# A fused two-layer kernel with Mish on one core: two x tiles by DMA transpose, and half of the first weight load issued later

## The chip, the cores and the metric

The kernel runs on one core of a Trainium2 chip. The metric is the device time of one execution in microseconds (us). Five engines work beside each other: TensorE (PE in the profile; its weight loads are PEld), VectorE (DVE), ScalarE (ACT), GpSimd (POOL) and SyncE (SP). Each runs its own instructions in order and waits on semaphores. SP and ScalarE also hand transfers to the 16 DMA engines, each through a queue of its own.

## What is computed

x is 2048 x 512, w1 is 512 x 1792, b1 has 1792 elements, w2 is 1792 x 512; all are bf16.

```python
h = jnp.einsum("bsd,df->bsf", x, w1) + b1
sp = jnp.log1p(jnp.exp(-jnp.abs(h))) + jnp.where(h > 0, h, jnp.zeros_like(h))
act = h * jnp.tanh(sp)            # Mish
return jnp.einsum("bsf,fd->bsd", act, w2)
```

## The kernel before

The 2048 rows of x are cut into four blocks of 512 rows. For each block the first layer is computed transposed: for each of 14 tiles f of 128 hidden columns, four matmuls (k = 0 to 3, the four parts of 128 of the inner dimension 512) add up in one PSUM bank, with the weights w1[k, f] stationary and x transposed streaming (512 columns). ScalarE applies Mish with the bias and writes a_sb (line 156). Then the second layer: for each of the block's four row tiles i, fourteen matmuls over f (line 189) with 512 columns of w2, a copy by VectorE (line 195), and a store issued on SP (line 198). All loads are issued at the start; nothing is loaded twice.

x is needed transposed (the tensor xT: 128 partitions of the inner dimension, by k, by row). Blocks 1 to 3 get it by a DMA transpose, issued on SP after all other loads (line 113, through the helper at line 84). Block 0 is needed first and gets it by TensorE: its four row tiles of 128 rows (x0 to x3 below) are loaded plainly into x_nat on SP (x0, x1 singly, x2 and x3 in one load, lines 101 to 103), transposed by TensorE into PSUM in four pieces of 128 x 128 each (`transpose_x`, line 134, transposes at line 144), and copied to xT by VectorE and ScalarE in turn (line 148).

w1 for the first four f (F0 = 4) is loaded on ScalarE's queue in two halves of 256 KB, k 0-1 and then k 2-3 (lines 99 and 100). Behind the x tiles, SP's queue has b1 (line 104), w1 for f 4-7 and for f 8-13 (lines 105, 106), w2 whole (line 107) and the three DMA transposes.

Around the change the order of the work is written out by hand (lines 214 to 239). TensorE first runs six matmuls on constants (line 127), then transposes x0, then alternates: `first(js, ks)` computes, for the four f of F0, the parts k in `ks` of the row tiles in `js`, in PSUM banks 4 to 7. So k 0 of x0 is done while x1 is not there yet, and 512 columns are put together from pieces of 128 and 256. The order before is:

```python
first((0,), (0,)); transpose_x(1); first((0,), (1,)); first((1,), (0, 1)); first((0, 1), (2,))
transpose_x(2); transpose_x(3); first((0, 1), (3,)); first((2, 3), (0, 1))
# bias: 14 x 128 transposed by TensorE (line 231)
first((2, 3), (2, 3))
```

When k 3 of the last row tile is done, Mish follows for that f. Then come f 4 to 13 in 512 columns (line 237) and the second layer of block 0 (line 239). The waits in the code are explicit: `Stream.wait` puts a semaphore wait into the engine's own instruction order, so what stands behind it on that engine waits too.

Of the kernel before, what the change touches and what calls it, by code (L numbers as in the profile page):

```python
# [5 lines left out]
P = 128  # L6
# [25 lines left out]
def bass_standalone__dense_activation_mish__prompt_kernel(  # L32
# [10 lines left out]
    BF, F32 = dt.bfloat16, dt.float32  # L43

    _, S, D = x.shape
    F = w1.shape[1]
    KT, FT = D // P, F // P
    assert (S, D, F) == (2048, 512, 1792) and sum(BLOCKS) == S
    x2, out2 = x[0], out[0]
# [3 lines left out]
    F0 = 4  # L53
    N0 = BLOCKS[0] // P

    with ExitStack() as es:
        def sb(name, shape, t):
            return es.enter_context(nc.sbuf_tensor(name, shape, t))

        x_nat = sb("x_nat", [P, N0, D], BF)  # L60
        xT = sb("xT", [P, KT, S], BF)
        w1_sb = sb("w1_sb", [P, KT, F], BF)
        w2_sb = sb("w2_sb", [P, FT, D], BF)
# [9 lines left out]
        def sem(name):  # L73
            return es.enter_context(nc.semaphore(name))

        sp = Stream(nc.sync, None)
        pe = Stream(nc.tensor, sem("c_pe"))
        dve = Stream(nc.vector, sem("c_dve"))
        act = Stream(nc.scalar, sem("c_act"))
        pool = Stream(nc.gpsimd, sem("c_pool"))  # L80

        def load(q, dst, src, name, transpose=False):
            s = sem(name)
            (q.eng.dma_start_transpose if transpose else q.eng.dma_start)(dst, src).then_inc(s, 16)
            return (s, 16)

        def load_w1(q, ks, a, b):
            return load(q, w1_sb[:, ks, a * P:b * P], w1v[:, ks, a * P:b * P], "s_w1_%d_%d" % (ks.start, a))


        t_xn, t_w1, t_w2 = [None] * N0, {}, {}

        def load_part(q, k0, k1, a, b):
            t = load_w1(q, slice(k0, k1), a, b)
            for f in range(a, b):
                for k in range(k0, k1):
                    t_w1[k, f] = t

        for k0, k1 in ((0, 2), (2, 4)):
            load_part(act, k0, k1, 0, F0)  # L100
        for j in range(2):
            t_xn[j] = load(sp, x_nat[:, j, :], x2[j * P:(j + 1) * P, :], "s_xn%d" % j)
        t_xn[2] = t_xn[3] = load(sp, x_nat[:, 2:4, :], x2[2 * P:4 * P, :].rearrange("(j p) d -> p j d", p=P), "s_xn2")
        t_b1 = load(sp, b1_nat[:, :], b1.rearrange("(j p) -> j p", p=P), "s_b1")
        load_part(sp, 0, KT, 4, 8)
        load_part(sp, 0, KT, 8, FT)
# [21 lines left out]


        free = [[] for _ in range(8)]  # L130
        t_cp = {}
        t_mish = {}

        def transpose_x(j, banks):

            pe.wait(t_xn[j], t_id)
            n = KT // len(banks)
            for h, bank in enumerate(banks):
                eng = (dve, act)[h % 2]
                pe.wait(*free[bank])  # L140
                psb = ps[:, bank, 0:n * P // 2].bitcast(BF)
                for i in range(n):
                    k = n * h + i
                    mm = nc.tensor.transpose(psb[:, i * P:(i + 1) * P], x_nat[:, j, k * P:(k + 1) * P], ident[:, :])  # L144
                eng.wait(pe.mark(mm))
                dst = xT[:, n * h:n * h + n, j * P:(j + 1) * P]
                src = psb.rearrange("p (k t) -> p k t", k=n)
                t = eng.mark(nc.vector.tensor_copy(dst, src) if eng is dve else act.eng.activation(dst, src, ACT.Copy))  # L148
                for i in range(n):
                    t_cp[j, n * h + i] = t  # L150
                free[bank] = [t]

        def mish(s, f, bank, t_mm):
            n = BLOCKS[s]
            act.wait(t_b1c, t_mm)
            t = act.mark(act.eng.activation(a_sb[:, f, starts[s]:starts[s + 1]], ps[:, bank, 0:n], ACT.Mish,  # L156
                                            bias=b1_sb[:, f:f + 1]))
            t_mish[s, f] = t
            free[bank] = [t]

        def mm1_step(s, f, k, bank, js=None):

            n = BLOCKS[s]
            lo, hi = (0, n) if js is None else (js[0] * P, (js[-1] + 1) * P)
            first = k == 0 and lo == 0
            if first:
                pe.wait(*free[bank])
            pe.wait(t_w1[k, f])
            if s:
                pe.wait(t_xT[s])  # L170
            else:
                pe.wait(*[t_cp[j, k] for j in (js or range(N0))])
            return nc.tensor.matmul(ps[:, bank, lo:hi], w1_sb[:, k, f * P:(f + 1) * P],  # L173
                                    xT[:, k, starts[s] + lo:starts[s] + hi], start=first, stop=(k == KT - 1 and hi == n))
# [32 lines left out]
        def first(js, ks):  # L207
            for k in ks:
                for f in range(F0):
                    mm = mm1_step(0, f, k, 4 + f, js)  # L210
                    if k == KT - 1 and js[-1] == N0 - 1:
                        mish(0, f, 4 + f, pe.mark(mm))
# [4 lines left out]
        dummy(256)  # L217
        first((0,), (0,))
        transpose_x(1, (0, 1))
        first((0,), (1,))  # L220
        first((1,), (0, 1))
        first((0, 1), (2,))
        transpose_x(2, (2, 3))
        transpose_x(3, (0, 1))
        dve.wait(t_b1, t_bz)
        t_b1p = dve.mark(nc.vector.tensor_copy(b1_pad[0:FT, :], b1_nat[:, :]))  # L226
        first((0, 1), (3,))
        first((2, 3), (0, 1))
        pe.wait(t_b1p, *free[2])
        psb1 = ps[:, 2, 0:P // 2].bitcast(BF)  # L230
        t_b1t = pe.mark(nc.tensor.transpose(psb1, b1_pad[:, :], ident[:, :]))  # L231
        dve.wait(t_b1t)
        t_b1c = dve.mark(nc.vector.tensor_copy(b1_sb[:, :], psb1[:, 0:FT]))  # L233
        free[2] = [t_b1c]
        first((2, 3), (2, 3))
        for f in range(F0, FT):
            mm1(0, f, {4: 0, 5: 1, 6: 2, 7: 3}.get(f, 4 + f % 4))
        for i in range(N0):
# [40 lines left out]
```

## Time and profile before

| | us |
|---|---|
| median of 3 runs | 106.08 |
| lowest and highest | 105.43, 106.5 |
| the profiled execution, its own time | 105.33 |
| its span, first to last instruction | 104.1 |
| TensorE busy in the span | 101.2 |
| ScalarE busy | 40.4 |
| VectorE busy | 12.8 |

The profile is one execution. The span is shorter than the time of the execution by 1.2 us, which lies around the instructions. Times within the profile count from the start of the span. A row of the timeline gives start, length, engine, line, operation and what it writes and reads, with the idle time before it and what ended that idle time. The chain of work that ended last is followed back from the last instruction, at each step to what released it; its pieces are listed in order of time. A busy TensorE is not TensorE at its peak, since matmuls overlap in its pipeline: the rate is read from the start of one to the start of the next.

### The profile page before, as it was taken

How to read it: one execution, taken by the hardware profiler on the slowest of the kernel's cores; microseconds unless marked ns; L12 is line 12 of the kernel's file. 1: busy time of each engine (PE TensorE's matmuls, PEld its weight loads, DVE VectorE, ACT ScalarE, POOL GpSimd, SP SyncE). 2: the span in 40 equal slices, each digit the busy share in tenths (PEclk: the TensorE clock that was granted, in tenths of full speed). 3: DMA queues.
4: the chain of work that ended last, by engine and by line, in shares of the span. 5: the costliest groups of instructions: out<-in, count | busy, mean ns of one | idle time of the engine just before them, and what ended most of it. 6: DMA issues, size and time to landing. Idle time of an engine off the chain costs nothing.

```text
span 104.1 us, 1166 instructions
## 1 busy us (share of the span) xinstructions
PE 101.2 (97%) x510; PEld 48.1 (46%) x510; DVE 12.8 (12%) x25; ACT 40.4 (39%) x62; POOL 0.7 (1%) x6
## 2 busy tenths in 40 slices
PE   6999999999999999999999999999999999999992
PEld 2486444444444444444444444444444444444462
DVE  0220000022220000022220000022112000011223
ACT  3426987000027777200007777500005777700000
POOL 2000000000000000000000000000000000000000
DMA  2999999941101000010111000001111000001111
GB/s 66 337 341 378 349 202 210 270 122 50 45 6 50 0 0 6 0 50 3 48 50 50 0 3 0 6 0 50 50 50 50 0 0 0 0 6 50 50 50 50
DMA packets 12689, 7.94 MB, mean 76 GB/s; under 512 B 6796, under 2 KB 12684, under 8 KB 12684
## 3 DMA queue, kind: packets, MB, share of 16 engines
q1 hardware_dynamic: 12140, 7.35, 25.6%
q10 hardware_dynamic: 544, 0.52, 1.5%
q8 instruction: 4, 0.07, 0.2%
q14 instruction: 1, 0.01, 0.0%
HBM read 4.20 MB, written 2.10 MB: 60 GB/s over the span
## 4 chain that ended last, share of the span: by engine, by line
PE 94%; DMA 3%; DVE 1%; issue 0%
PE ps L173 47%; PE ps L189 47%; DMA w_sb<-in_w_dram 3%; PE ps L144 1%; DVE xT L148 0%; DVE o_sb L195 0%; PE ps L231 0%
## 5 line engine op out<-in xcount | busy, mean ns | idle before, releaser
L156 ACT ACTIVATE a_sb<-ps,b_sb 128x512 bf16<-128x512 f32 x56 | 37.6, 690 | 46.1 <-PE ps L173 46.0
L173 PE MATMUL ps<-xT,w_sb 128*128 128x512 bf16 (+2 forms) x248 | 49.7, 359 | 0.2
L189 PE MATMUL ps<-w_sb,a_sb 128*128 128x512 bf16 (+2 forms) x238 | 49.0, 367 | 0.0
L173 PEld LDWEIGHTS ps<-xT,w_sb 128*128 128x128 bf16 x248 | 23.4, 98 | 25.4 <-DMA w_sb<-in_w_dram 0.4
L189 PEld LDWEIGHTS ps<-w_sb,a_sb 128*128 128x128 bf16 x238 | 22.8, 98 | 25.9
L195 DVE CAST o_sb<-ps 128x512 bf16<-128x512 f32 (+2 forms) x17 | 11.2, 660 | 83.0 <-PE ps L189 83.0
L127 PE MATMUL ps<-const-bfloat16-1.0 128*128 128x512 bf16 (+1 forms) x7 | 2.9, 557 | 0.8 <-PEq L264 0.8
L148 ACT ACTIVATE xT<-ps 128x256 bf16<-128x256 bf16 (+1 forms) x5 | 1.5, 340 | 2.5 <-PE ps L144 2.5
L121 ACT ACT_TABLE_LOAD x1 | 1.3, 1283 | 1.8 <-issue 1.8
L148 DVE COPY xT<-ps 128x256 bf16<-128x256 bf16 (+1 forms) x5 | 1.2, 265 | 4.6 <-PE ps L144 4.6
L127 PEld LDWEIGHTS ps<-const-bfloat16-1.0 128*128 128x128 bf16 x7 | 0.9, 135 | 1.9 <-issue 1.9
L144 PE MATMUL ps<-ident,x_nat 128*128 128x128 bf16 x16 | 1.6, 243 | 0.0
L144 PEld LDWEIGHTS ps<-ident,x_nat 128*128 128x128 bf16 x16 | 1.1, 108 | 0.7 <-DMA x_nat<-in_x_dram 0.7
L233 DVE CAST b_sb<-ps 128x14 f32<-128x14 bf16 x1 | 0.2, 173 | 1.2 <-PE ps L231 1.2
L119 POOL TENSOR_SCALAR_AFFINE_SELECT ident<-ones 128x128 bf16<-128x128 bf16 x1 | 0.3, 292 | 0.1
L116 DVE MEMSET b_pad<- 128x64 uint32 x1 | 0.1, 112 | 0.9 <-PEq L264 0.9
L231 PE MATMUL ps<-ident,b_pad 128*128 128x128 bf16 x1 | 0.2, 219 | 0.0
L117 POOL MEMSET ones<- 128x128 bf16 x1 | 0.2, 204 | 0.3 <-POOLq L264 0.3
L226 DVE COPY b_pad<-b_nat 14x128 bf16<-14x128 bf16 x1 | 0.2, 173 | 0.0
L231 PEld LDWEIGHTS ps<-ident,b_pad 128*128 128x128 bf16 x1 | 0.1, 98 | 0.0
L264 POOL MEMSET const-bfloat16-1.0<- 128x1 bf16 x1 | 0.1, 101 | 0.0
L264 POOL MEMSET const-uint8-127<- 128x1 uint8 x1 | 0.1, 101 | 0.0
(2 smaller groups left out, 0.2 us busy)
## 6 DMA issues: line engine op xcount, KB each, us to landing
out_dram<-o_sb SPq DMA_DIRECT2D x15, 128.0 KB, 1.7
w_sb<-in_w_dram SPq DMA_DIRECT2D x1, 1792.0 KB, 12.7
w_sb<-in_w_dram SPq DMA_DIRECT2D x1, 768.0 KB, 7.2
w_sb<-in_w_dram ACTq DMA_DIRECT2D x2, 256.0 KB, 3.7
w_sb<-in_w_dram SPq DMA_DIRECT2D x1, 512.0 KB, 5.5
x_nat<-in_x_dram SPq DMA_DIRECT2D x2, 128.0 KB, 2.7
x_nat<-in_x_dram SPq DMA_DIRECT2D x1, 256.0 KB, 4.0
out_dram<-o_sb SPq DMA_DIRECT2D x1, 96.0 KB, 1.6
```

Of the source, the lines that this page charges most:

```text
L117: t_ones = pool.mark(pool.eng.memset(ones[:, :], 1.0))
L119: t_id = pool.mark(pool.eng.affine_select(ident[:, :], ones[:, :], pattern=[[1, P]], compare_op=ALU.is_equal, fill=0.0, base=0, channel_mu ...
L121: act.eng.preload_act_table(ACT.Mish)
L127: nc.tensor.matmul(ps[:, 7, 0:n], c_w, c_m[:, 0:n], start=True, stop=True)
L144: mm = nc.tensor.transpose(psb[:, i * P:(i + 1) * P], x_nat[:, j, k * P:(k + 1) * P], ident[:, :])
L148: t = eng.mark(nc.vector.tensor_copy(dst, src) if eng is dve else act.eng.activation(dst, src, ACT.Copy))
L156: t = act.mark(act.eng.activation(a_sb[:, f, starts[s]:starts[s + 1]], ps[:, bank, 0:n], ACT.Mish, bias=b1_sb[:, f:f + 1]))
L173: return nc.tensor.matmul(ps[:, bank, lo:hi], w1_sb[:, k, f * P:(f + 1) * P], xT[:, k, starts[s] + lo:starts[s] + hi], start=first, stop=( ...
L189: return nc.tensor.matmul(ps[:, bank, 0:hi - lo], a_sb[:, f, i * P:(i + 1) * P], w2_sb[:, f, lo:hi], start=(f == 0), stop=(f == FT - 1))
L195: t = dve.mark(nc.vector.tensor_copy(o_sb[:, i, lo:hi], ps[:, bank, 0:hi - lo]))
L226: t_b1p = dve.mark(nc.vector.tensor_copy(b1_pad[0:FT, :], b1_nat[:, :]))
L231: t_b1t = pe.mark(nc.tensor.transpose(psb1, b1_pad[:, :], ident[:, :]))
```

## The change

x2 and x3 of block 0 are no longer loaded plainly, transposed by TensorE and copied. One DMA transpose, the third transfer on SP's queue, writes both into xT; x_nat keeps two tiles. ScalarE issues only k 0-1 of w1 at the start; the issue of k 2-3 stands behind the copies of x0 and x1 in ScalarE's order, with a wait for the landing of k 0-1. In the order of the work, k 0-1 is done in pieces as before (x0, x1, then x2 and x3 together), and k 2 and k 3 in 512 columns for all four row tiles, with the bias transpose between them.

```diff
-        x_nat = sb("x_nat", [P, N0, D], BF)
+        x_nat = sb("x_nat", [P, 2, D], BF)
...
-        for k0, k1 in ((0, 2), (2, 4)):
-            load_part(act, k0, k1, 0, F0)
+        load_part(act, 0, 2, 0, F0)
         for j in range(2):
             t_xn[j] = load(sp, x_nat[:, j, :], x2[j * P:(j + 1) * P, :], "s_xn%d" % j)
-        t_xn[2] = t_xn[3] = load(sp, x_nat[:, 2:4, :], x2[2 * P:4 * P, :].rearrange("(j p) d -> p j d", p=P), "s_xn2")
+        t_x23 = load(sp, xT[:, :, 2 * P:4 * P], x2[2 * P:4 * P, :], "s_x23", True)
         t_b1 = load(sp, b1_nat[:, :], b1.rearrange("(j p) -> j p", p=P), "s_b1")
...
-        t_cp = {}
+        t_cp = {(j, k): t_x23 for j in (2, 3) for k in range(KT)}
...
         first((0,), (0,))
         transpose_x(1, (0, 1))
+        act.wait(t_w1[0, 0])
+        load_part(act, 2, 4, 0, F0)
         first((0,), (1,))
         first((1,), (0, 1))
-        first((0, 1), (2,))
-        transpose_x(2, (2, 3))
-        transpose_x(3, (0, 1))
         dve.wait(t_b1, t_bz)
         t_b1p = dve.mark(nc.vector.tensor_copy(b1_pad[0:FT, :], b1_nat[:, :]))
-        first((0, 1), (3,))
         first((2, 3), (0, 1))
+        first(range(N0), (2,))
         pe.wait(t_b1p, *free[2])
...
-        first((2, 3), (2, 3))
+        first(range(N0), (3,))
```

More of the change, by code (lines that the diff above doesn't have):

```diff
@@ L88, in load_w1 @@
             return load(q, w1_sb[:, ks, a * P:b * P], w1v[:, ks, a * P:b * P], "s_w1_%d_%d" % (ks.start, a))
-        t_xn, t_w1, t_w2 = [None] * N0, {}, {}
+        t_xn, t_w1, t_w2 = [None] * 2, {}, {}
         def load_part(q, k0, k1, a, b):
```

## The prediction

> **What bounds the kernel now.** I read the page first, then the chain of work that ended last.
>
> ```profile
> PE 101.2 (97%) x510; PEld 48.1 (46%) x510; DVE 12.8 (12%) x25; ACT 40.4 (39%) x62; POOL 0.7 (1%) x6
> ...
> PE 94%; DMA 3%; DVE 1%; issue 0%
> ```
>
> TensorE is busy for 97% of the span, and the chain is TensorE but for 3% of DMA. So only what TensorE has to do, or has to wait for, can move the end. The chain in order of time shows where its waits lie:
>
> ```profile
> 0.80 3.21 DMA w_sb<-in_w_dram
> 4.01 0.04 issue
> 4.05 0.40 PE ps L173 x4
> ...
> 4.47 0.30 PE ps L144 x2
> ...
> 4.79 0.30 DVE xT L148
> ...
> 5.14 1.06 PE ps L173 x12
> 6.20 0.45 PE ps L144 x8
> 6.64 1.40 PE ps L173 x12
> 8.04 0.06 PE ps L231
> 8.10 9.51 PE ps L173 x48
> 17.60 12.09 PE ps L189 x56
> 29.69 12.09 PE ps L173 x56
> ```
>
> From 5.14 on TensorE never stops. All that the change touches lies before 8.97, where the last 40 of the 48 matmuls at 8.10 begin (f 4 to 13, 512 columns each). One 512-column matmul costs 12.09/56 = 0.216 us, so one of 256 columns costs 0.108. What happens to the end is the shift of the moment, now 17.60, at which the second layer begins. The queues that feed this, from the timeline:
>
> ```profile
> 0.80 0.99 ACTq L84 DMA_DIRECT2D w_sb<-in_w_dram  x2
> 0.81 1.35 SPq L84 DMA_DIRECT2D x_nat<-in_x_dram  x3
> ...
> 2.74 1.50 SPq L84 DMA_DIRECT2D w_sb<-in_w_dram  x3
> ...
> 4.27 15.76 SPq L84 DMA_TRANSPOSE xT<-in_x_dram  x3
> ...
> 4.90 0.38 ACT L148 ACTIVATE xT<-ps 128x256 bf16<-128x256 bf16 x1 [0.82 <-PE ps L144]
> 5.14 0.78 PEld L173 LDWEIGHTS ps<-xT,w_sb 128*128 128x128 bf16 x12 [0.22 <-DVE xT L148]
> ```
>
> The three issues from 2.74 (w1 for f 4-7, w1 for f 8-13, w2) are 0.5 apart: 2.74, 3.24, 3.74. Issue rows say when an engine hands a transfer over, not when it lands. Landings are in the page's DMA part, and in the views of the tiles w_sb, x_nat and xT, each with the least, median and longest:
>
> ```profile
> w_sb<-in_w_dram SPq DMA_DIRECT2D x1, 1792.0 KB, 12.7
> w_sb<-in_w_dram SPq DMA_DIRECT2D x1, 768.0 KB, 7.2
> w_sb<-in_w_dram ACTq DMA_DIRECT2D x2, 256.0 KB, 3.7
> w_sb<-in_w_dram SPq DMA_DIRECT2D x1, 512.0 KB, 5.5
> ```
> ```profile
> DMA to landing us min/median/max: 3.2/5.5/12.7
> ```
> ```profile
> DMA to landing us min/median/max: 2.3/3.2/4.0
> ```
> ```profile
> L84 SPq DMA_TRANSPOSE xT<-in_x_dram x3: 2027/2613/11032, 4.3 to 18.0; - x3
> ...
> DMA to landing us min/median/max: 4.1/4.8/14.0
> ```
>
> The two 256 KB loads of w1 on ScalarE's queue average 3.7; the first took 3.2 (0.80 to 4.01), so the second, k 2-3, took 4.2 and was there at about 5.5. TensorE first needs it at about 5.7. Today it is hidden.
>
> **The change part by part.**
>
> TensorE's work. The eight transposes of x tiles 2 and 3 go. Sixteen 256-column matmuls of k 2-3 become eight of 512: the same columns, so nothing. If no transfer were late, TensorE would go on at 5.14 with eight 128-column matmuls (their weight loads: 0.78/12 = 0.065 each, 0.52), be at 5.66, do x tiles 2-3 with k 0-1 (8 x 0.108 = 0.86), k 2, the bias transpose (0.06) and k 3 (8 x 0.216 = 1.73) and start f 4 at 8.31 instead of 8.97: a gain of 0.65. That is the most the removed work is worth. The four copies removed from VectorE and ScalarE lie beside TensorE and are worth nothing on the path. ScalarE's first queue stretch loses one issue (0.5), so its table load moves up; nothing waits for that.
>
> The start. Can x0, x1 and k 0-1 (512 KB) land sooner without the other loads?
>
> ```profile
> 1.60:3.20 1.60, 1.60 (x6) 0.51 (x5) 0.00 (x0) 1.28 (x1) 0.00 (x0) 1.00 0.76 228
> 3.20:4.00 0.80, 0.74 (x6) 0.41 (x5) 0.44 (x2) 0.41 (x2) 0.00 (x0) 1.00 1.01 337
> ```
>
> By 3.2 us 228 x 1.6 = 365 KB had moved; the 524 (thousand bytes) of these three need until 3.67 even if nothing else ran. So k 0-1 gains between 0 and 0.3. They were already first in their queues, and I take 0.
>
> x tiles 2-3 by DMA transpose, issued third on SP, at 1.73. Landing: the rows for double the bytes are 4.1 to 4.8, with less than 1 us to save for half the bytes. Bounds 3.2 and 4.8; I take 4.1, the row without other work before it: 5.8. TensorE then does the k 0-1 part until 5.83 + 0.86 = 6.7.
>
> SP's queue. The issue replaces one of 0.43; three issues of 512 rows took 2.0, 2.6 and 11.0, so half as many rows cost about 1.3, and between 0.4 and 2.7 (if, like the 11.0, it ends only when the data ahead is out, here near 4.4). Everything behind it on SP (bias, w1 for f 4-7 and 8-13, w2, the other transposes) is issued 0.9 later, bounds 0 to 2.3. On the wire these follow one another anyway. What changes there is a seam: at the one place where transposed data follows plain data now, the DMA engines moved almost nothing for 2 us.
>
> ```profile
> 14.50:15.00 0.50, 0.50 (x4) 0.21 (x3) 0.00 (x0) 0.37 (x1) 0.00 (x0) 1.00 0.83 65
> 15.00:15.50 0.50, 0.50 (x5) 0.20 (x3) 0.00 (x0) 0.45 (x1) 0.00 (x0) 1.00 2.92 36
> 15.50:16.00 0.50, 0.50 (x4) 0.27 (x3) 0.00 (x0) 0.32 (x2) 0.00 (x0) 1.00 0.08 8
> 16.00:16.50 0.50, 0.50 (x4) 0.22 (x3) 0.00 (x0) 0.50 (x1) 0.00 (x0) 1.00 0.45 96
> 16.50:18.00 1.50, 1.50 (x9) 0.69 (x7) 0.00 (x0) 1.15 (x3) 0.00 (x0) 1.00 1.28 288
> ```
>
> The last number is GB/s. So every later transfer lands 0.2 us (262 thousand bytes at 288 instead of 360 or so) to 2.2 later; after only 2 us of traffic I take 0.6. w2 now lands at 3.74 + 12.7 = 16.4 and is first used at 17.60: 1.2 of cover. w1 for f 4-7 lands at 2.74 + 5.5 = 8.2 and is used at 8.97: 0.7. Both uses move later too (below), so both stay hidden; without that move w2 at its upper bound, 18.6, would be next to stop TensorE. The bias copy on VectorE waits for a small load that now lies behind the transpose; its consumer comes after k 2, so it is hidden.
>
> k 2-3 on ScalarE. This is the term that decides. ScalarE works in order: the wait for k 0-1 and the issue stand behind its copy of x1, which ended at 4.90 + 0.38 = 5.28. By then k 0-1 has long landed, so the wait itself is free, but the load is issued at 5.28 instead of 1.3. Behind it on ScalarE is nothing until the first activation. Landing: 2.3 is the lowest row of any load here (half the bytes), 4.2 the same load in traffic; the nearest is k 0-1, same queue and size, 3.2. So 5.28 + 3.2 = 8.5, bounds 7.6 and 9.4.
>
> [...]
>
> The sum. TensorE waits from 6.7 to 8.5, then has 48 x 0.216 + 0.06 = 10.43 to do: second layer at 8.52 + 10.43 = 18.95 instead of 17.60, +1.35. Seen from the gain of 0.65, the late k 2-3 costs 2.0. The profiled execution took 105.33, with a span of 104.1, 0.75 under the median of 106.08; 105.33 + 1.35 = 106.7, and against the median 107.4. Break-even is a landing of k 2-3 at 17.60 - 10.43 - 0.04 = 7.13. With the bounds 7.6 and 9.4 this case runs from 106.5 to 108.4.
>
> **The rivals.**
>
> Early: k 2-3 lands before 7.6. For it: x1's copy may end up to 0.3 earlier, and TensorE has 0.65 to give back. Against it: 7.13 would need 1.85 from issue to landing, less than any load row. It decides below 7.13: no slower, at best 105.4, which is the end on the other side; between 7.13 and 7.6 up to 106.5.
>
> Backlog: the load is served in order of issue after SP's earlier ones. Behind w1 for f 8-13, which now lands at 3.24 + 7.2 = 10.4 and would land 0.2 to 0.8 later, it lands at 10.6 to 11.2: +3.5 to +4.1, 109.6 to 110.2. For it: x0, k 0-1, x1 and k 2-3 landed (3.1, 4.0, 4.4, 5.5) in about the order of issue. [...]
>
> Blocked issue: SP's first transpose for block 1 stays in issue for 11.0 us, until 15.3. If ScalarE can issue nothing during it, k 2-3 lands at 15.5 + 3.2 = 18.7, +11.6: 117.7. It decides if that transpose starts before ScalarE's 5.28; it starts at 4.27 now, 5.2 by my shift, up to 6.6. Landing behind w2 instead gives 16.6 and 115.5. Against it: the issues of ScalarE and SP at 0.80 and 0.81 ran side by side. [...]
>
> Clock: TensorE stands idle for 1.8 us and comes back slow.
>
> ```profile
> 1.22 0.15 PEld L127 LDWEIGHTS ps<-const-bfloat16-1.0 128*128 128x128 bf16 x1 [0.28 <-issue]
> 1.65 0.15 PEld L127 LDWEIGHTS ps<-const-bfloat16-1.0 128*128 128x128 bf16 x1 [0.28 <-issue]
> ```
>
> At the start the 512-column matmuls follow each other at 0.43, half speed, until somewhere before 4.05: up to 3.2 us, a loss of half of it, 1.6. Then 109.0. [...]
>
> **How the numbers follow.** Chances: forecast 0.58, early 0.10, backlog 0.10, blocked or behind w2 0.14, clock 0.08. The time is that of the likeliest, 107.4. The range 106.3 to 110.2 holds the forecast's own range (106.5 to 108.4), clock, backlog and the upper half of early; left out are 0.14 and about 0.05. A measurement here can tell about 1% (1.06 us) from no change. Slower by over 1% means a landing after 8.19: 0.34 of the forecast's 0.58, and backlog, blocked and clock, 0.66. Faster by over 1% would need more than the whole 0.65 and a sooner start: 0.02. The rest, 0.32, is within 1%.
>
> **What the changed profile would show.** Right: a wait of TensorE for w_sb of 1 to 3 us, ending near 8.5, ahead of the first 512-column matmul of line 173 in block 0; ScalarE's second issue near 5.3; no other new wait; the second layer at about 18.9. The transposed x tiles land between 4.9 and 6.5; later than 7.6 would make them the wait instead. Wrong: no wait for w_sb and the second layer at 17.0 (early); a landing past 10 (backlog, blocked); 512-column matmuls 0.43 apart after the wait (clock); a wait for w_sb at line 189 (w2's cover gone).

## The result, and the profile after

The changed kernel takes 113.23 us (median of 4 runs, 112.62 to 113.81) against 106.22 for the kernel before (4 runs): 1.069 times as long, 95% interval 1.064 to 1.074. The forecast was 107.4 with a range of 106.3 to 110.2. Ratios, here and below, leave out single runs that lay more than 1.5% above the fastest of their kernel. The profiled execution took 112.77, its span is 111.5 (before: 105.33 and 104.1).

From the profile of the changed kernel: busy time, the row of the granted TensorE clock by slices of 2.8 us, and the shares of the chain.

```profile
PE 103.6 (93%) x494; PEld 48.3 (43%) x494; DVE 12.4 (11%) x23; ACT 40.2 (36%) x60; POOL 0.7 (1%) x6
...
PEclk9997559999999999999999999999999999999999
...
PE 91%; DMA 6%; DVE 0%; issue 0%; ACT 0%
```

TensorE fell from 97% to 93% of the span, and a row for the clock has appeared: seven, five and five tenths between about 8 and 17 us. The chain in order of time says where the span grew.

```profile
5.20 0.01 ACT xT L147
5.20 7.23 DMA w_sb<-in_w_dram
...
12.48 1.89 PE ps L172 x4
14.36 0.11 PE ps L229
14.47 10.53 PE ps L172 x44
25.00 12.09 PE ps L188 x56
```

The second layer of block 0 begins at 25.00 instead of 17.60: 7.40 later, which is the whole growth of the span (111.5 - 104.1). From 25.00 on every piece has the length that it had before. Ahead of it there is one wait: k 2-3 of w1 is issued at 5.20 and lands at 12.43, 7.2 us later. The waits name the same thing, and their totals show that there is no other new wait for data on TensorE.

```profile
PEld ps L172 <- DMA w_sb<-in_w_dram: 5.9, 2, 5.5
PE ps L172 <- DMA w_sb<-in_w_dram: 5.2, 1, 5.2
```

The second part of the loss is what happens after the wait. The timeline of the weight loads:

```profile
12.47 0.13 PEld L172 LDWEIGHTS ps<-xT,w_sb 128*128 128x128 bf16 x2 [5.50 <-DMA w_sb<-in_w_dram]
...
12.88 0.15 PEld L172 LDWEIGHTS ps<-xT,w_sb 128*128 128x128 bf16 x1 [0.28 <-issue]
13.30 0.15 PEld L172 LDWEIGHTS ps<-xT,w_sb 128*128 128x128 bf16 x1 [0.28 <-issue]
```

They follow each other at 0.42, where a 512-column matmul at full clock takes 0.216. The stretches of the windows view (PE busy, PEld, DVE, ACT, POOL, granted clock, DMA share, GB/s) show from when to when:

```profile
7.00:7.30 0.30, 0.26 (x3) 0.00 (x0) 0.00 (x0) 0.00 (x0) 0.00 (x0) 1.00 1.06 375
7.30:9.00 1.70, 0.00 (x0) 0.00 (x0) 0.00 (x0) 0.00 (x0) 0.00 (x0) 1.00 1.06 382
9.00:10.00 1.00, 0.00 (x0) 0.00 (x0) 0.00 (x0) 0.00 (x0) 0.00 (x0) 0.80 1.07 387
10.00:11.00 1.00, 0.00 (x0) 0.00 (x0) 0.00 (x0) 0.00 (x0) 0.00 (x0) 0.50 1.07 349
...
14.00:16.40 2.40, 2.40 (x8) 0.86 (x7) 0.17 (x1) 1.40 (x3) 0.00 (x0) 0.50 1.23 277
16.40:17.60 1.20, 1.20 (x7) 0.61 (x6) 0.00 (x0) 1.20 (x3) 0.00 (x0) 0.99 1.18 267
```

TensorE stopped at 7.26; the clock fell to half at about 9.6 (0.80 is the mean of a stretch that is full for six tenths of it) and came back at 16.4. Note the last column as well: during TensorE's wait the DMA engines move 350 to 390 GB/s. They are not idle; they are moving something else.

The sum with these numbers: TensorE needs 10.43 after the landing at full clock, 12.48 + 10.43 = 22.91, so the clock cost 25.00 - 22.91 = 2.09 (with the restart after the wait, some 0.16 of it: with the clock kept, the same work takes 10.59 in an experiment below, 12.89 to 23.48). The landing came 12.43 - 8.48 = 3.95 later than forecast. Forecast shift 1.35 + 3.95 + 2.09 = 7.39.

What was moved in that time, from the list of issues with size and time to landing, and SP's issues:

```profile
w_sb<-in_w_dram SPq DMA_DIRECT2D x1, 1792.0 KB, 11.9
w_sb<-in_w_dram SPq DMA_DIRECT2D x1, 768.0 KB, 6.8
...
w_sb<-in_w_dram SPq DMA_DIRECT2D x1, 512.0 KB, 4.9
```
```profile
1.73 1.31 SPq L84 DMA_TRANSPOSE xT<-in_x_dram  x1
...
3.74 1.50 SPq L84 DMA_DIRECT2D w_sb<-in_w_dram  x3
...
5.20 0.37 ACTq L84 DMA_DIRECT2D w_sb<-in_w_dram  x1
5.29 15.56 SPq L84 DMA_TRANSPOSE xT<-in_x_dram  x3
```

w1 for f 4-7 is issued at 3.74 and lands at 8.6, w1 for f 8-13 is issued at 4.19 and lands at 11.0, w2 is issued at 4.73 and lands at 16.6. ScalarE's load comes after all three, lands behind two of them and ahead of the third. That is the suspicion with which the experiments begin.

### The profile page after: what moved, and what is told of

It reads as the page before. It is cut to its first block, busy times and chain, and to the rows that moved or that the text cites. A ratio compares the mean times of both kernels' runs of the same rounds, so it can differ in the third digit from the quotient of the medians.

```text
span 111.5 us, 1128 instructions
## 1 busy us (share of the span) xinstructions
PE 103.6 (93%) x494; PEld 48.3 (43%) x494; DVE 12.4 (11%) x23; ACT 40.2 (36%) x60; POOL 0.7 (1%) x6
## 4 chain that ended last, share of the span: by engine, by line
PE 91%; DMA 6%; DVE 0%; issue 0%; ACT 0%
PE ps L172 44%; PE ps L188 43%; DMA w_sb<-in_w_dram 6%; PE ps L126 2%; PE ps L143 1%; DVE o_sb L194 0%; PE ps L229 0%; ACT xT L147 0%
## 5 line engine op out<-in xcount | busy, mean ns | idle before, releaser
L155 ACT ACTIVATE a_sb<-ps,b_sb 128x512 bf16<-128x512 f32 x56 | 38.1, 688 | 54.6 <-PE ps L172 54.4
L172 PE MATMUL ps<-xT,w_sb 128*128 128x512 bf16 (+2 forms) x240 | 52.2, 380 | 5.2 <-DMA w_sb<-in_w_dram 5.2
L172 PEld LDWEIGHTS ps<-xT,w_sb 128*128 128x128 bf16 x240 | 23.9, 103 | 32.3 <-DMA w_sb<-in_w_dram 5.9
L194 DVE CAST o_sb<-ps 128x512 bf16<-128x512 f32 (+2 forms) x17 | 11.2, 660 | 84.1 <-PE ps L188 84.1
L147 ACT ACTIVATE xT<-ps 128x128 bf16<-128x128 bf16 (+1 forms) x3 | 0.9, 314 | 2.1 <-PE ps L143 2.1
L147 DVE COPY xT<-ps 128x128 bf16<-128x128 bf16 (+1 forms) x3 | 0.7, 247 | 3.5 <-PE ps L143 3.5
```

What stands on the lines that cost most here:

```text
L194: t = dve.mark(nc.vector.tensor_copy(o_sb[:, i, lo:hi], ps[:, bank, 0:hi - lo]))
```

## The experiments

Two theories: **backlog** (what SP has handed over earlier is moved first, whichever queue the later load uses) and **transpose** (the new DMA transpose in front is what holds the load up). The clock is a third matter, tested by itself. In the diffs, `rest of SP` stands for the loads of w1 for f 4-13, w2 and the three block transposes. Where a kernel was timed only once, the text says so, and what is read there is the landing in its profile.

**Undo the late issue, keep the DMA transpose.**

```diff
+        load_part(act, 2, 4, 0, F0)          # right behind k 0-1 at the start
...
-        act.wait(t_w1[0, 0])
-        load_part(act, 2, 4, 0, F0)
```

> The changed kernel with both halves of w1 for f 0-3 issued on ScalarE at the start again; x2 and x3 still by DMA transpose. Theory backlog (a load of ScalarE is moved only after what SP had handed over before it): no wait for w1; the transposed x tiles stand behind k 2-3 on the wire and land near 6.4 instead of 5.8, the second layer begins at 17.6 to 17.9, time 105.8 to 106.8. Theory transpose (the DMA transpose of the x tiles holds up what comes after it): TensorE waits for w1 of f 4-7 near 9, and the time is above 107.

Measured: 105.77 (10 runs) against 106.20, ratio 0.997 (0.994 to 0.9995). The chain of this kernel has no wait for w1 after the start:

```profile
5.14 3.37 PE ps L173 x24
8.50 0.06 PE ps L228
8.56 9.50 PE ps L173 x44
18.06 12.09 PE ps L189 x56
```

The second layer stands at 18.06 in this execution, a little past the expected 17.9; the median lies at the lower end of what was expected. That the layer begins later here than in the profile before (17.60), while the median is no longer, fits the matmul rates of the two executions: here the matmuls run at half rate until 7.0, in the profiled execution before only until somewhere before 4.05. So the DMA transpose, with everything that it moves on SP's queue, costs nothing that can be measured. The whole loss belongs to the late issue, as the next kernel shows.

**The late issue alone, in the kernel before.**

```diff
-        for k0, k1 in ((0, 2), (2, 4)):
-            load_part(act, k0, k1, 0, F0)
+        load_part(act, 0, 2, 0, F0)
...
         transpose_x(1, (0, 1))
+        act.wait(t_w1[0, 0])
+        load_part(act, 2, 4, 0, F0)
```

> The kernel before with one edit: k 2-3 of w1 is issued behind the copies of x1 with the wait for k 0-1. No DMA transpose for block 0. Theory backlog: k 2-3 lands after w1 for f 8-13 again, between 10 and 13; TensorE needs it at 5.7, so the second layer moves by 4.5 to 7 and more with a slow clock: 111 to 115. Theory transpose: without the early DMA transpose it lands 3.2 after its issue, near 8.5, +2.8: about 109.

Measured: 113.96, ratio 1.075 (1.069 to 1.082). There is no DMA transpose of x tiles in this kernel, and the load still takes 6.75:

```profile
4.85 6.75 DMA w_sb<-in_w_dram
...
26.33 12.09 PE ps L188 x56
```

It also answers the question of the blocked issue. SP's first block transpose was handed over at 4.28, before ScalarE's load, and stayed in issue for 11.5 us (view of xT: the least, median and longest issue in ns, first and last start):

```profile
L84 SPq DMA_TRANSPOSE xT<-in_x_dram x3: 1916/2012/11491, 4.3 to 17.8; - x3
```

ScalarE issued at 4.85, in 0.37, and its load landed at 11.60: SP's stuck issue did not stop it.

The theory transpose falls. The loss is as large as that of the whole change.

**SP holds its large loads until ScalarE has issued k 2-3.**

```diff
         act.wait(t_w1[0, 0])
         load_part(act, 2, 4, 0, F0)
+        sp.wait(t_cp[1, 2])                  # ScalarE's copy of x1
+        rest of SP                           # moved here from the start
```

> The changed kernel, but SP hands over w1 for f 4-13, w2 and the block transposes only when ScalarE's copy of x1 is done, which is just after ScalarE has issued k 2-3. Theory backlog: k 2-3 lands 2.6 to 3.2 after its issue, at 7.9 to 8.5, the second layer at 18.4 to 19.0, time 107.0 to 107.7 (the forecast's own case). Theory transpose (the x tiles' DMA transpose, still ahead, is what holds it up): it lands past 10 again and the time stays above 110.

Measured: 106.79 (9 runs), ratio 1.008 (1.004 to 1.011). The load is as late as in the changed kernel (here 5.57), behind the same DMA transpose, on the same queue. Only what lies ahead of it is gone:

```profile
5.57 2.80 DMA w_sb<-in_w_dram
...
19.03 12.09 PE ps L179 x56
```

2.8 instead of 7.2. That is the backlog, shown by removing it. It is also the case that the forecast had assumed, and the time lies inside that case's own range (106.5 to 108.4), though a little under the 107.0 that I expected here: the medians differ by 0.6, while the second layer is 1.43 later than in the profile before, which is of a short execution (105.33).

**How much of the backlog counts.** Three kernels, each timed once: with only w1 for f 4-7 ahead of the load, then w1 for f 4-13, then w2 in the place of w1 for f 8-13:

```diff
# first: hold from w1 for f 8-13 on; second: hold from w2 on (as above, sp.wait later in SP's order)
# third, nothing held:
         load_part(sp, 0, KT, 4, 8)
-        load_part(sp, 0, KT, 8, FT)
         t = load(sp, w2_sb[:, :, :], w2v, "s_w2")
+        load_part(sp, 0, KT, 8, FT)
```

> The changed kernel, but SP hands over w1 for f 8-13 and all behind it only after ScalarE's copy of x1; only w1 for f 4-7 (512 KB) is ahead of k 2-3. Theory limited order (the DMA engines work off what was handed over first, up to a certain number of pieces, and only then take turns between the two queues): k 2-3 lands after w1 for f 4-7, at 8.2 to 8.9. Theory turns (the queues take turns at once, and it is the sheer number of bytes in flight that slows the load): 7.8 to 8.2, ahead of w1 for f 4-7.

> As the run before, but w1 for f 4-7 and for f 8-13 (1280 KB) are both ahead of k 2-3, and only w2 is held. Theory limited order: k 2-3 lands after w1 for f 8-13, and sooner than the 12.4 of the changed kernel, where it shared with w2: 10.7 to 11.7. Theory turns: 7.8 to 8.5, as in the run before.

> The changed kernel with w2 handed over on SP before w1 for f 8-13; only the landing of k 2-3 is looked at, TensorE then waits for w1 as well. Theory limited order by pieces (ahead of k 2-3 lie w1 for f 4-7 and f 8-13, 64 pieces for each DMA engine, and w2 is where the sharing began): now w1 for f 4-7 and the first two sevenths of w2 are ahead, smaller pieces, so k 2-3 starts earlier, shares with the rest of w2 and lands at 11.0 to 12.0. Theory order by whole transfers (two are worked off, the third shares): behind all of w2, 14 or later.

Measured, the load's row in the chain of each of the three, in this order:

```profile
5.06 3.99 DMA w_sb<-in_w_dram
```
```profile
5.32 6.54 DMA w_sb<-in_w_dram
```
```profile
5.29 7.82 DMA w_sb<-in_w_dram
```

Issue to landing is 2.8 with nothing ahead, 4.0 behind 512 KB (landing 9.05, after w1 for f 4-7 at 3.74 + 4.6 = 8.3), 6.5 behind 1280 KB (11.86, after w1 for f 8-13 at 4.19 + 6.6 = 10.8), 7.2 with w2 behind them as well. Both landings are some 0.15 past what limited order gave. The theory that the two queues take turns from the start, which gave 7.8 to 8.5 for the first two, falls.

The traces also record every packet with its queue and its start, and they show what the landings hide. The load's first packet starts 1.0 us after the issue with nothing ahead, 2.0 behind 512 KB, 3.8 behind 1280 KB and 4.0 in the changed kernel (at 9.2). From then on its packets start among SP's: in the changed kernel 76 of its packets and 87 of SP's start between 10.0 and 10.5, its last one at 11.8.

In the third, order by whole transfers would have been 14 or later, and the load came at 13.1, before w2 (4.19 + 10.2 = 14.4): it does share with a part of what is ahead. But my estimate by the number of pieces, 11.0 to 12.0, was missed by a microsecond, so at what point the sharing begins stays open. No single number of pieces fits: SP had started some 350 packets of its large loads before the load's first one behind 512 KB, and about 880 to 1060 in the other two kernels and the changed one. The times were 107.46, 111.96 and 113.40.

**The same load on SP, at the same place in the order** (timed once):

```diff
         load_part(sp, 0, KT, 8, FT)
+        load_part(sp, 2, 4, 0, F0)           # and not on ScalarE, without the wait
```

> The changed kernel with k 2-3 handed over on SP, behind w1 for f 8-13 and ahead of w2, near 4.7, half a microsecond sooner than ScalarE did it. Theory order of handing over: it lands right behind w1 for f 8-13, 11.2 to 11.9, so ScalarE's own queue brought nothing. Rival (ScalarE's queue is served worse than SP's): it lands well before 11, between 8 and 10.

Measured: handed over at 4.73, landed at 12.29, against 12.43 from ScalarE's queue at 5.20.

```profile
4.73 7.56 DMA w_sb<-in_w_dram
```

It lands 0.4 later than I said, but nowhere near 8 to 10: a queue of its own brought the load nothing.

**The wait and the issue earlier in ScalarE's order.**

```diff
         dummy(256)
+        act.wait(t_w1[0, 0])
+        load_part(act, 2, 4, 0, F0)
         first((0,), (0,))
         transpose_x(1, (0, 1))
-        act.wait(t_w1[0, 0])
-        load_part(act, 2, 4, 0, F0)
```

> The changed kernel with the wait and the issue of k 2-3 moved ahead of x1's transposes in ScalarE's order: issued near 4.1, when k 0-1 has landed, before SP has handed over w2 and about when it hands over w1 for f 8-13. Theory limited order: behind w1 for f 4-7, perhaps shared with f 8-13: lands at 8.3 to 9.5, the second layer begins at 18.8 to 20, the time is 107.2 to 108.5. Theory turns or a fixed price per load: 3.2 to 7.2 after the issue means either 7.3 (105.9 to 106.4) or 11.3 (111 to 112).

Measured: 109.1 (107.94 to 110.53 in 4 runs), ratio 1.028 (1.022 to 1.035, without the 110.53); issued at 3.90, landed 5.2 later at 9.1 as expected. But it did not land behind w1 for f 4-7, as I had expected: that load, handed over 0.16 before it, landed at 3.74 + 5.7 = 9.4. Handed over almost together, the two shared the way.

```profile
w_sb<-in_w_dram SPq DMA_DIRECT2D x1, 512.0 KB, 5.7
...
3.90 5.20 DMA w_sb<-in_w_dram
```

The time is above my 107.2 to 108.5, and the second layer, at 21.43, is 1.4 past the expected 20. TensorE waited only 2.1 us here, and yet the clock fell:

```profile
PEclk9997699999999999999999999999999999999999
```

In the kernel with 512 KB ahead TensorE waited 2.3 us and that row is full throughout. The shorter wait cost the clock and the longer one did not, and executions of this one kernel differ too: two of its four have a mean granted clock of 0.984, the other two of 1.000.

**The clock by itself.** The changed kernel with matmuls on constants in the wait:

```diff
         first((2, 3), (0, 1))
+        pe.wait(*free[3])
+        for _ in range(20):
+            nc.tensor.matmul(ps[:, 3, :], c_w, c_m, start=True, stop=True)
         first(range(N0), (2,))
```

> The changed kernel with 20 matmuls of 512 columns on constants in the wait for k 2-3 (into a PSUM bank that is free then; results unused). Both theories on the landing: it stays at 12 to 12.7. If the clock was the second part of the loss (2.1 of 7.4 us), the 512-column matmuls after the wait follow each other at 0.216 at once, the second layer begins near 22.9 instead of 25.0 and the time is 111.1. If the slow start after the wait has another cause, 113.2 stays.

Measured: 111.34, ratio 1.050 (1.046 to 1.055), 1.9 under the changed kernel (in ratios 1.050 and 1.069) and 0.2 above the expected 111.1, though the load landed even later (5.52 + 7.33 = 12.85):

```profile
5.52 7.33 DMA w_sb<-in_w_dram
...
12.89 1.04 PE ps L172 x4
13.93 0.06 PE ps L232
13.98 9.50 PE ps L172 x44
23.48 12.09 PE ps L188 x56
```

Four 512-column matmuls take 1.04 instead of 1.89, and 44 take 9.50 instead of 10.53. The clock's share of the loss, about 1.9, is shown.

**Toward a better version.** k 2-3 on SP right behind the transposed x tiles; and, from the first experiment, both halves at the start with k 2 and 3 of x0 and x1 done before x2 and x3 are needed:

```diff
# on SP (and not on ScalarE, without the wait)
+        load_part(sp, 2, 4, 0, F0)           # behind t_x23, ahead of t_b1
# at the start (load_part(act, 2, 4, 0, F0) right behind k 0-1, as in the first experiment): order of the pieces
-        first((2, 3), (0, 1))
-        first(range(N0), (2,))
+        first((0, 1), (2, 3))
+        first((2, 3), (0, 1))
...
-        first(range(N0), (3,))
+        first((2, 3), (2, 3))
```

> The changed kernel with k 2-3 handed over on SP right behind the x tiles' DMA transpose, near 3.1, ahead of all large loads. Theory order of handing over: it is moved right behind the transposed tiles and lands at 6.4 to 7.2, about when TensorE needs it (6.7): 105.6 to 106.4. Rival (a load behind a DMA transpose is held up by it): it lands past 8 and the time is above 107.

> Both halves of w1 for f 0-3 at the start and x2 and x3 by DMA transpose, as in the first experiment; in addition k 2 and 3 of x0 and x1 are done (256 columns) before x2 and x3 are needed, so that 0.86 us of TensorE work covers the landing of the transposed tiles near 6.1. Theory: nothing is waited for after 5.2, the gain of 0.65 us for the eight removed transposes comes out whole: 105.3 to 105.7, against 106.2 for the kernel before. Rival: the four removed waits were free and the transposes were hidden by the clock's slow start: 105.8 to 106.2, as in the first experiment or before.

Measured, against 105.60 for the kernel before, run beside them: on SP 105.96 (10 runs), ratio 1.002 (0.9998 to 1.0045); with the pieces 105.49 (12 runs), ratio 0.998 (0.996 to 1.001). Neither can be told from the kernel before, although 105.96 and 105.49 lie in what was expected: the kernel before was 105.60 here and not 106.2. On SP, k 2-3 landed 3.5 after its issue at 3.09, at 6.6, as order of handing over had it, and the next load became the wait: w1 for f 4-7, issued at 4.25.

```profile
4.25 4.64 DMA w_sb<-in_w_dram
...
8.94 8.81 PE ps L173 x40
17.74 12.09 PE ps L189 x56
```

With the pieces TensorE had no wait after x1's landing, and the 0.65 still did not come out:

```profile
1.25 3.64 DMA x_nat<-in_x_dram
...
4.93 0.61 PE ps L144 x4
5.54 3.10 PE ps L173 x28
8.64 0.06 PE ps L228
8.69 9.51 PE ps L173 x48
18.20 12.09 PE ps L189 x56
```

In this execution x1 landed at 4.89 (4.43 before), the four transposes of x1 took 0.61 (0.40 before), and 28 matmuls that by the prediction's rates cost 12 x 0.065 + 16 x 0.108 = 2.51 took 3.10. So here a later x1 and slow early matmuls ate the gain. The matmuls are slow because the slow start lasted longer: their starts in the trace are at half rate until 6.8, and before only until somewhere before 4.05. But 105.97 was this execution's time, the longest of the twelve, and where the slow start ends differs from trace to trace here, from before 4.05 to 7.0. Whether the gain comes out in the median run can't be read from one profile, and stays open.

## Why the prediction was wrong, point by point

**The bound and the break-even: right.** Only the start of the second layer mattered, and its shift, 7.40, is the growth of the span.

**x tiles by DMA transpose: right.** Forecast landing 5.8; it was issued at 1.73, and in the view of xT the shortest landing is 4.1, which gives 5.8. Its consumer was done at 7.26 instead of 6.7, because the matmuls ran at half rate until 6.2, which the wait hid. The forecast took the rates from a profile whose slow start ended by 4.05. The issue took 1.31, as worked out from half of 2.6, and SP's loads moved by 1.0 (0.9 forecast). w2 and w1 for f 4-7 stayed hidden, behind the longer wait. That this half of the change costs nothing is shown by the first experiment; that its gain of 0.65 comes out whole is not, the best measured is 0.3% with an interval that ends at 0.05%.

**The time of the late issue: right.** 5.20, forecast 5.28, behind x1's copy; the wait itself was free. (The upper bound of the landing, 5.28 + 4.2, is 9.48 and not 9.4, and 15.5 in the blocked case stands where the long issue ends at 15.3; neither changes the outcome.)

**"The nearest is k 0-1, same queue and size, 3.2": the step that failed.** The landing of k 2-3, forecast at 8.5, came at 12.43: from issue to landing 7.2 instead of 3.2. Size and queue were the wrong likeness. The row of 3.2 belongs to a load that was handed over first, with nothing ahead of it. I had the number that decides in a quoted row, 512 + 768 + 1792 KB handed over on SP from 2.74 on, and gave the rival backlog a chance of 0.10; that the load would not stand behind these was shown by no row of the profile before. At some 360 GB/s those first two alone are 3.6 us, an estimate from the rate in the windows. The hold experiment, where nothing is ahead, gave 2.8 and 106.79: the term was right for an empty road, and the road was full.

Behind 512 KB and behind 1280 KB the load landed after what was ahead, at 9.05 after 8.3 and at 11.86 after 10.8, because its first packet started 2.0 and 3.8 us after its issue. In the changed kernel that was 4.0 us; from 9.2 on its packets started among those of SP, and it landed at 12.43, ahead of w2 at 16.6.

**The rival backlog: right in kind, too low in price.** Forecast landing 10.6 to 11.2, measured 12.43. w1 for f 8-13 landed at 11.0, as that rival had it; the price gave the load itself nothing on top. It took 1.4 us more here, and 1.1 with w2 held (11.86 against 10.8), where its 256 KB alone are 0.7 at 360 GB/s, an estimate; the rest fits the packets of w2 that started among its own (in the changed kernel 83 of SP's 87 between 10.0 and 10.5 were w2's). The chance of 0.14 for "blocked or behind w2" went to cases that did not come: the load passed w2, and issue was not blocked. In the kernel with the late issue alone, ScalarE's issue at 4.85 fell into SP's long one and took 0.37.

**The clock: priced as a rival of its own, when it follows from the other.** I gave 1.6 and 0.08, for a wait of 1.8 us; no row of the profile before shows the clock after a wait. In all five profiles with a wait of 4.8 us or more and no matmuls on constants in it, the clock fell; backlog and clock together are one case, 110.2 + 1.6 = 111.8 by my own terms, and the range should have reached it. Even that is 1.4 short of 113.23: the landing was 1.2 later than the backlog's latest, and the clock cost 2.09 instead of 1.6.

## What to carry to other kernels

A load's time from issue to landing did not follow from its size or queue here (2.8 to 7.8 us for the same 256 KB): read what has been handed over before it and is still to be moved, and add that first. To move a load later was to move it behind most of what the other queue had been handed in the meantime; if a load is to go late on purpose, hold the others as well. And a wait on TensorE can bring the clock with it, here in one of two profiles with a wait of about 2 us (2.1 and 2.3) and in all five with 4.8 us or more and no matmuls on constants in it, at a cost of 2.09 us in the changed kernel, so both belong in one case. A profile is one execution: before its early matmuls are used as rates or as a baseline, look where its slow start ends.

## What the runs showed of the hardware that was not expected

In the changed kernel the clock fell 2.3 us after TensorE's last matmul (7.26 to about 9.6) and returned 3.9 us after its first (12.48 to 16.4):

```profile
7.26:9.61 2.35, 0.00 (x0) 0.00 (x0) 0.00 (x0) 0.00 (x0) 0.00 (x0) 1.00 1.05 382
9.61:16.43 6.82, 3.95 (x11) 1.48 (x12) 0.17 (x1) 1.43 (x3) 0.00 (x0) 0.50 1.13 325
```

With waits of 2.1 and 2.3 us it fell in one kernel's profile, that of the shorter wait, and not in the other's. Why, and how long a wait has to be to cost the clock, was not shown.

During the first warm-up matmuls, 0.43 apart, the granted clock reads 1.00, although 512-column matmuls are 0.216 apart later on at 1.00: in the profiles before and after the change that column does not show the slow start. In the kernel with w2 in the place of w1 for f 8-13, SP's issue of w1 for f 8-13 took 2.8 us instead of 0.5 (three issues in 3.79, from 3.74): a plain load was held in issue too, here with 512 and 1792 KB ahead of it.

```profile
3.74 3.79 SPq L84 DMA_DIRECT2D w_sb<-in_w_dram  x3
```
